# Storing x^T of a block in 384-byte pieces, reading low words on VectorE and sharing one set of buffers in an attention-and-softplus kernel

## The chip, the core and the metric

The kernel runs on one core of a Trainium2 chip. The metric is the device time of one execution in microseconds (us). Before the change it is 929.13 us, the median of three runs (928.65 to 930.0). The profile below is of another execution of the same kernel, with a span of 926.7 us from the first to the last instruction.

## The reference

Two blocks follow each other. The first is linear attention with a norm over each head; the second is a feed-forward layer with softplus between its two products.

```python
# q, k, v: (8 batches, 8 heads, 576 tokens, 64), g_norm: (64,)
kv  = einsum('bhsd,bhse->bhde', k, v)
o   = einsum('bhsd,bhde->bhse', q, kv)
o   = o / sqrt(mean(o * o, axis=-1) + 1e-6) * g_norm
x   = o.transpose(0, 2, 1, 3).reshape(4608, 512)
# moe_w_in: (512, 2048), moe_w_out: (2048, 512)
h   = x @ moe_w_in
g   = maximum(h, 0) + log1p(exp(-abs(h)))
out = g @ moe_w_out              # (4608, 512), float32
```

The weights arrive as 64-bit numbers (`wide` in the code): each is a low and a high 32-bit word, which the kernel turns into one float32.

## The kernel before

TensorE multiplies in a reduced float format (`F32R`), so each operand is divided into three parts (`[:, 0]`, `[:, 1]`, `[:, 2]`), and every product is a sum of three. The 4608 tokens are 12 blocks of 384 tokens, each three tiles of 128. The 2048 hidden columns are 16 chunks of 128. One step is one chunk of one block: 12 matmuls of 384 columns (`mm1`), softplus on ScalarE, a division of the result on ScalarE and VectorE, and 9 matmuls of 512 columns (`mm2`). There are 192 steps in three phases; in each phase a block takes only some of the chunks, because only 8 chunks' weights are resident, and a partial sum per tile goes to DRAM between phases.

No scheduler orders the instructions at run time: the Python class `Plan` lays every task on its engine's queue beforehand, from a guessed duration, a position (`pos`, in steps) and rings of buffers. A task that needs a buffer is put where the plan expects one to be free. The table `P0` holds the tuned positions. Where the plan expects a gap on TensorE before the first step, it puts a matmul that is thrown away (`warm`).

```python
    rings = dict(xv=2, gv=2, g=2, raw=2, lf=1, sq=1, t=1, p=1, w=1,
                 tail0=1, tail1=1, xt=2, kvt=6, qa=1, qT=2, x=2, xg=2, r=2,
                 h=2, o=2, tp=1, s0=1, s1=1, s2=1)
    # weight(): one weight tile of 128 x 512 numbers of two words each
            a1 = add("ACT", 670, square, [f], pos, [sq], [raw])
            a2 = add("ACT", 670, low, [f], pos, [lf], [raw])       # L289: lf <- low words
            d1 = add("DVE", 430, high1, [f], pos, [t], [raw])      # L292
            d2 = add("DVE", 690, high2, [d1], pos, [], [raw])      # L296
            d3 = add("DVE", 690, mask, [d2, a1], pos, [])          # L301
            ...
            d4 = add("DVE", 430, power, [d3], pos, [p, w])         # L309
            d5 = add("DVE", 690, rest, [d4, a2], pos, [], [lf])    # L314: p <- lf * p
            ready = add("DVE", 690, total, [d3, d5], pos, [], [t, p])  # L317
    # divide(): the weight's three parts; for the first chunks the third by TensorE (L368, L369)
    # split(): three parts of a tile of x^T, for mm1
        def high():                                                # L438, ACT
            nc.scalar.activation(cols(0, F32R), x.tile, func=AF.Identity, scale=g_down)
        def low():                                                 # L441, DVE
            nc.vector.scalar_tensor_tensor(out=cols(1, F32R), in0=x.tile, scalar=g_col, in1=cols(0), ...)
        def less():                                                # L445, DVE
            ...
    # kv_of(b): four pieces and a tail of k and v; L491 loads k, L493 v, L483/L485 the tails; L507 matmuls
    # load_q(b): from batch 2 on, q comes in runs of 128 bytes (L416), turned by VectorE (L554);
    # in batches 0 and 1 it comes in rows (L569) and is turned by TensorE (L579)
    # rows(t): attention of tile t
        a = o_task = add("PE", ..., out_rows, ...)                 # L524: o <- kv_diag, qT
        a = add("ACT", 600, <Square of o>, [a], pos, [x])          # L592
        a = add("DVE", 690, reduce, [a], pos, [r])                 # L529
        a = add("POOL", 2300, root, [a], pos)                      # L532, L533
        a = add("DVE", 700, norm, [a, o_task], pos, [], [o, r])    # L536
        if t < BY_PE:                                              # BY_PE = 12
            a = add("PE", 440, turn_x, [a], pos + 0.5, [xp], [x])  # L541
            if t < AT_ONCE:
                split(0, t, xp, a, pos + 0.5)
            ...                                                    # L601 copy, L602 store of x^T
            return
        def turn_blocks():                                         # L608: 32 x 32 blocks
            nc.vector.transpose(out=new(xg, [P, d_model]), in_=x.tile.rearrange("p h d -> p (h d)"))
        def store(r0):                                             # L611
            nc.sync.dma_start(out=xd[t][:, r0:r0 + BL].rearrange("(b i) j -> i b j", i=BL),
                              in_=xg.tile[r0:r0 + BL].rearrange("i (b j) -> i b j", j=BL))
        a = add("DVE", 690, turn_blocks, [a], pos, [xg], [x])
        x_there[t] = [add("SP", 450, lambda r0=r0: store(r0), [a], pos + 0.5, [], [xg], 450)
                      for r0 in range(0, P, BL)]
    # x_again(): x^T of a tile loaded from DRAM (L620) and split, in every phase
    # step(): mm1 L642, softplus L662, first part L664, second L653, third L657, mm2 L649
    # leave(): a tile's sum leaves its bank: L683 (phase 0) or L689, then a store L693
    # warm(): L747
```

Of the kernel before, what the change touches and what calls it, by code (L numbers as in the profile page):

```python
# [40 lines left out]
class Plan:  # L41
# [13 lines left out]
    def slot(self, ring):  # L55
        return Slot(ring)
# [10 lines left out]
    def order(self):  # L67
# [15 lines left out]
        while left:  # L83
            best = None
            for engine, tasks in ready.items():
                options = []
                for t in tasks:
                    at = max(engine_free[engine], t.ready)
                    if t.size:
                        at = max(at, dma_free - 2500)  # L90
                    for s in t.take:
                        if not free[s.ring]:
                            break
                        at = max(at, min(free[s.ring])[0])
# [47 lines left out]
def kernel(  # L142
# [41 lines left out]

    P0 = [-44.5, 1.3, -27.8, -10.7, -15.1, 4.5, -20.4, -2.8, -54.5, -31.8, -31.7, -9.2, -25.2, -1.2,
          27.3, -6.2, 3.0, -12.0, 8.5, 9.5, 5.0, 21.5, -1.5, 2.5, 2.5, 27.0, -6.5, 13.0, 9.0, 44.5,
          49.5, 67.5, 56.5, 71.5, 95.5, 100.5, 115.0, 112.0, 116.5, 9.0]
    CONVERT, FETCH, EARLY, LATER = P0[:8], P0[8:16], P0[16:27], P0[27:]
# [21 lines left out]

    rings = dict(xv=2, gv=2, g=2, raw=2, lf=1, sq=1, t=1, p=1, w=1,
                 tail0=1, tail1=1, xt=2, kvt=6, qa=1, qT=2, x=2, xg=2, r=2,
                 h=2, o=2, tp=1, s0=1, s1=1, s2=1)
# [44 lines left out]
    def weight(j, pos, fetch_pos):  # L258
# [8 lines left out]
        c, of_out = divmod(j, 2)  # L267
        raw, w = slot("raw"), slot("w")
        words = 2 if wide else 1
# [8 lines left out]
        if wide:  # L278
            sq, lf, t, p = (slot(n) for n in ("sq", "lf", "t", "p"))

# [3 lines left out]
            def square():  # L284
                nc.scalar.activation(new(sq, [P, d_model], BF16), raw.tile.bitcast(BF16)[:, :, 3],
                                     func=AF.Square, scale=2.0 ** 47)

            def low():
                nc.scalar.activation(new(lf, [P, d_model]), words_of()[0], func=AF.Copy, scale=2.0 ** -52)  # L289

# [21 lines left out]
            def rest():  # L312
                pf = p.tile.bitcast(F32)
                nc.vector.tensor_tensor(out=pf, in0=lf.tile, in1=pf, op=ALU.mult)  # L314

# [4 lines left out]
            a1 = add("ACT", 670, square, [f], pos, [sq], [raw])  # L320
            a2 = add("ACT", 670, low, [f], pos, [lf], [raw])
            d1 = add("DVE", 430, high1, [f], pos, [t], [raw])
# [3 lines left out]
            d4 = add("DVE", 430, power, [d3], pos, [p, w])  # L326
            d5 = add("DVE", 690, rest, [d4, a2], pos, [], [lf])
            ready = add("DVE", 690, total, [d3, d5], pos, [], [t, p])
# [3 lines left out]
        if c < PLACES or first_step[c] - last_step[c - PLACES] > 12:  # L332
            divide(j, w, ready, pos, "p", c < 4)
        else:
            spilled = dram.tile([P, d_model], F32, name=f"w_spill{j}")
            st = add("SP", 350, lambda: nc.sync.dma_start(out=spilled, in_=w.tile), [ready], pos, [], [w], 900)
            again = slot("x" if of_out else "qT")
# [3 lines left out]
            divide(j, again, ld, back, "xg")  # L341

# [54 lines left out]
    first_tile = [b * S // P for b in range(B)]  # L397
    xd = [dram.tile([d_model, P], F32, name=f"x{t}") for t in range(n_tiles)]
    x_there = {}
# [6 lines left out]
    def load_q(b):  # L406


        q_slots[b], q_loads[b] = slot("qa"), []
        pos = x_pos(first_tile[b] + 1) - EARLY[7]  # L410

        def run(e, c):
            if not (e or c):
                new(q_slots[b], [P, NP * S])
            r0 = BL * (2 * e + c)
            nc.sync.dma_start(  # L416
                out=q_slots[b].tile[r0:r0 + BL].rearrange("j (i d) -> j i d", d=BL),
                in_=q[b, e * NP:(e + 1) * NP, :, BL * c:BL * (c + 1)].rearrange("p (i j) d -> j (p i) d", j=BL))

        for e in range(2):  # L420
            for c in range(2):
                q_loads[b].append(add("SP", 450, lambda e=e, c=c: run(e, c), (), pos + 0.2 * (2 * e + c),
                                      [q_slots[b]] if not (e or c) else [], [], 2000, behind=int(pos) - 3,
                                      follows=q_loads[b][-1] if e or c else None))
# [41 lines left out]
    def kv_of(b):  # L466
# [5 lines left out]
        for p in range(NP + 1):  # L472
            tail = p == NP
            ks, vs = (slot(f"tail{i}" if tail else "kvt") for i in range(2))
            n = S - MAIN if tail else P

            def load(src, s, p=p, tail=tail, n=n, ks=ks):
# [14 lines left out]
                else:  # L492
# [3 lines left out]
                       620 if tail else size, behind=int(pos - 2) - 3)  # L496
                   for src, s, ns, size in ((k, ks, 900, 1250), (v, vs, 500, 900))]

# [18 lines left out]
    def rows(t):  # L517
        pos = x_pos(t)
        tp, qT, o, x, r, xp, xg = (slot(n) for n in ("tp", "qT", f"s{t}" if t < TB else "o", "x", "r", "tp", "xg"))
        def out_rows():  # L520
# [28 lines left out]
        for b, r0, n, s0 in parts(t):  # L549
# [12 lines left out]
            at_qa = n == P and b == 0  # L562
            q_s = q_slots[0] if at_qa else slot("kvt")

# [32 lines left out]
        if t < BY_PE:  # L597
            a = add("PE", 440, turn_x, [a], pos + 0.5, [xp], [x])
            if t < AT_ONCE:
                split(0, t, xp, a, pos + 0.5)  # L600
            a = add("ACT", 600, lambda: nc.scalar.copy(new(xg, [P, KD, P]), xp.tile), [a], pos + 1, [xg], [xp])  # L601
            x_there[t] = [add("SP", 450, lambda: nc.sync.dma_start(  # L602
                out=xd[t].rearrange("(a p) t -> p a t", p=P), in_=xg.tile), [a], pos + 1, [], [xg], 950)]
            return


        def turn_blocks():
            nc.vector.transpose(out=new(xg, [P, d_model]), in_=x.tile.rearrange("p h d -> p (h d)"))  # L608

        def store(r0):  # L610
            nc.sync.dma_start(out=xd[t][:, r0:r0 + BL].rearrange("(b i) j -> i b j", i=BL),  # L611
                              in_=xg.tile[r0:r0 + BL].rearrange("i (b j) -> i b j", j=BL))

        a = add("DVE", 690, turn_blocks, [a], pos, [xg], [x])
        x_there[t] = [add("SP", 450, lambda r0=r0: store(r0), [a], pos + 0.5, [], [xg], 450) for r0 in range(0, P, BL)]

    def x_again(ph, t):
        pos = first_step[ph, t // TB] - EARLY[8] + 0.5 * (t % TB)
        xt = slot("xt")
        ld = add("SP", 350, lambda: nc.sync.dma_start(out=new(xt, [P, KD, P]), in_=xd[t].rearrange("(a p) t -> p a t", p=P)),  # L620
                 x_there[t], pos - EARLY[9], [xt], [], 900, behind=first_step[ph, t // TB] - 5)
        split(ph, t, xt, ld, pos)
# [56 lines left out]
    def leave(ph, t, bank, done, pos):  # L679

        ot = slot("xg" if ph == 0 else ("qT", "x", "xg")[t % TB] if ph == LAST else "qT")
        if ph == 0:
            a = add("ACT", 600, lambda: nc.scalar.activation(new(ot, [P, d_model]), bank.tile, func=AF.Copy, scale=1.0 + E),  # L683
                    [done], pos, [ot], [bank])
        else:
            pt = slot("kvt")
            ld = add("SP", 350, lambda: nc.sync.dma_start(out=new(pt, [P, d_model]), in_=part[ph - 1, t][0]),
                     [part[ph - 1, t][1]], pos - EARLY[10], [pt], [], 900, behind=int(pos) - 4)
            a = add("DVE", 700, lambda: nc.vector.scalar_tensor_tensor(  # L689
                out=new(ot, [P, d_model]), in0=bank.tile, scalar=(scale if ph == LAST else 1.0 + E), in1=pt.tile,  # L690
                op0=ALU.mult, op1=ALU.add), [done, ld] + (scale_done if ph == LAST else []), pos, [ot], [bank, pt])
        dst = out[t * P:(t + 1) * P] if ph == LAST else dram.tile([P, d_model], F32, name=f"part{ph}_{t}")
        st = add("SP", 350, lambda: nc.sync.dma_start(out=dst, in_=ot.tile), [a], pos, [], [ot], 900)  # L693
        part[ph, t] = dst, st

    def whole_scale(pos):

        if not wide:
            scale_done.append(add("DVE", 60, lambda: nc.vector.memset(scale, 1.0 + E), (), pos))
            return  # L700
        ones, total = slot("kvt"), slot("h")
        a = add("DVE", 130, lambda: nc.vector.memset(new(ones, [P, P]), 1.0), (), pos, [ones])
# [80 lines left out]
```

## Time and profile before

| what | value |
|---|---|
| device time, median of 3 | 929.13 us |
| span of the profiled execution | 926.7 us |
| TensorE clock granted | 1.000 |
| mm1, L642 | 2304 matmuls, first at 46.6 us |
| mm2, L649 | 1728 matmuls |
| thrown-away matmuls, L747 | 48, 17.9 us busy, all before 46.6 us |
| low words, L289 on ScalarE | 32, 666 ns each |
| x^T by 32 x 32 blocks, L608 on VectorE | 24, 709 ns each |
| its stores, L611 | 96 DMAs of 64 KB |
| DMA packets | 265219, of which 164289 under 512 B |

The names: PE is TensorE, PEld its loading of weights, DVE VectorE, ACT ScalarE, POOL GpSimd and SP (or SPq) the queue that issues the DMAs. A line such as `L642` is a line of the kernel before. In the page's second part the span is cut into 40 slices of 23.2 us, and a digit is the busy share of one slice in tenths. The page's fifth part has one row for each group of equal instructions: how many, their busy time in all, the mean length of one in nanoseconds, and the idle time of the engine just before them with what ended it. In a timeline each row is one instruction or a run of equal ones, with its start and its length in microseconds, and in brackets the idle time before it and what ended that.

Matmuls are pipelined, so the lengths of neighbours overlap, and the sum of their busy times can't be read as the time that they need.

### The profile page before, as it was taken

The numbers are of one execution on the slowest core, as the hardware profiler recorded it, in microseconds if no ns is written. First come the engines' busy times: TensorE is split into PE (matmuls) and PEld (weight loads), VectorE is DVE, ScalarE is ACT, GpSimd is POOL, SyncE is SP. The second block draws the span as 40 slices with busy tenths as digits, with TensorE's granted clock in tenths as the row PEclk, the third lists the DMA queues.
The fourth block names the chain that finished last, engine by engine and source line by source line (L and its number), as shares of the span: only waits on it lengthen the run. The fifth ranks groups of instructions, "written<-read, shape, count | busy, mean of one in ns | idle before, by whom it ended". The sixth has DMA issues, their size and how long they took to land.

```text
span 926.7 us, 13338 instructions
## 1 busy us (share of the span) xinstructions
PE 909.2 (98%) x4826; PEld 818.4 (88%) x4826; DVE 628.2 (68%) x1055; ACT 433.7 (47%) x831; POOL 83.6 (9%) x78
## 2 busy tenths in 40 slices
PE   7899999999999999999999999999999999999998
PEld 5689888998998999998989999999889999999997
DVE  6865877876466786888855877888644455555553
ACT  6865654553334555655533555657323233323231
POOL 0322332221122220000000000000000000000000
PEclk9999999999999999999999999999999999999999
DMA  8998989794976452454534434544221323333322
GB/s 227 245 203 225 155 205 198 186 194 111 167 164 145 103 147 81 159 160 159 163 122 135 127 125 147 171 155 144 84 85 57 103 95 122 114 102 103 103 80 103
DMA packets 265219, 131.44 MB, mean 142 GB/s; under 512 B 164289, under 2 KB 239041, under 8 KB 265153
## 3 DMA queue, kind: packets, MB, share of 16 engines
q1 hardware_dynamic: 264992, 130.59, 54.3%
q8 instruction: 38, 0.62, 0.3%
q14 instruction: 29, 0.23, 0.1%
q10 hardware_dynamic: 160, 0.00, 0.0%
HBM read 91.75 MB, written 38.80 MB: 141 GB/s over the span
## 4 chain that ended last, share of the span: by engine, by line
PE 88%; DMA 6%; SPq 2%; DVE 1%; ACT 1%; issue 1%; POOL 0%; ACTq 0%; DVEq 0%
PE s L649 41%; PE h L642 41%; PE o L524 3%; PE o L507 3%; DMA kvt<-in_v_dram 2%; DMA xt<-x 1%; SPq L611 1%; DMA qa<-in_q_dram 1%; DMA part<-xg 1%; DMA raw<-in_moe_w_in_dram 1%; SPq L416 0%; DMA g_col<-in_g_norm_dram 0%; PE h L747 0%; PE tp L541 0%; PE tp L579 0%
## 5 line engine op out<-in xcount | busy, mean ns | idle before, releaser
L649 PE MATMUL s<-w,gv 128*128 128x512 f32 x1728 | 435.1, 395 | 1.0 <-ACT xg L683 0.9
L642 PE MATMUL h<-xv,w 128*128 128x384 f32 x2304 | 434.1, 337 | 0.0
L642 PEld LDWEIGHTS h<-xv,w 128*128 128x128 f32 x2304 | 406.3, 188 | 14.7
L649 PEld LDWEIGHTS s<-w,gv 128*128 128x128 f32 x1728 | 319.1, 188 | 61.4 <-ACT xg L683 2.6
L662 ACT ACTIVATE g<-h 128x384 f32<-128x384 f32 x192 | 94.1, 490 | 336.3 <-PE h L642 335.3
L653 DVE TENSOR_TENSOR gv<-g,gv 128x384 fp32r<-128x384 f32 x192 | 106.5, 555 | 170.0 <-ACT gv L664 169.1
L664 ACT ACTIVATE gv<-g 128x384 fp32r<-128x384 f32 x192 | 100.8, 525 | 40.3 <-PE s L649 33.1
L657 DVE SCALAR_TENSOR_TENSOR gv<-gv 128x384 fp32r<-128x384 f32 x192 | 106.9, 557 | 6.2
L441 DVE SCALAR_TENSOR_TENSOR xv<-xt,g_col,xv 128x512 fp32r<-128x512 f32 x102 | 75.8, 744 | 5.4 <-ACT xv L438 5.3
L438 ACT ACTIVATE xv<-xt,g_down 128x512 fp32r<-128x512 f32 x102 | 72.3, 713 | 10.6 <-DMA xt<-x 10.4
L445 DVE SCALAR_TENSOR_TENSOR xv<-xv 128x512 fp32r<-128x512 f32 x108 | 74.4, 689 | 2.6
L533 POOL TENSOR_TENSOR r<-r,half 128x8 f32<-128x8 f32 x36 | 68.0, 1888 | 3.0
L507 PEld LDWEIGHTS o<-kvt,kvt 128*128 128x128 f32 x256 | 33.4, 196 | 9.3 <-issue 6.8
L507 PE MATMUL o<-kvt,kvt 128*128 128x128 f32 x256 | 35.3, 282 | 6.3 <-DMA kvt<-in_v_dram 6.2
L524 PE MATMUL o<-kv_diag,qT 128*128 128x128 f32 (+1 forms) x296 | 37.5, 277 | 1.1 <-DVE x L536 1.1
L524 PEld LDWEIGHTS o<-kv_diag,qT 128*128 128x128 f32 (+1 forms) x296 | 35.0, 179 | 3.7 <-PE o L507 1.4
L532 POOL TENSOR_SCALAR r<-r 128x8 f32<-128x8 f32 x36 | 14.9, 414 | 249.0 <-DVE r L529 248.9
L689 DVE SCALAR_TENSOR_TENSOR qT<-s,kvt 128x512 f32<-128x512 f32 x36 | 24.6, 686 | 11.6 <-PE s L649 11.1
L554 DVE STREAM_TRANSPOSE qT<-qa 128x512 f32<-128x512 f32 (+1 forms) x30 | 19.0, 646 | 18.0 <-DMA qa<-in_q_dram 7.6
L529 DVE TENSOR_REDUCE r<-x 128x8 f32<-128x512 f32 x36 | 24.4, 678 | 8.3 <-ACT x L592 8.3
L689 DVE SCALAR_TENSOR_TENSOR qT<-s,scale,kvt 128x512 f32<-128x512 f32 x12 | 9.0, 751 | 29.7 <-PE s L649 29.7
L592 ACT ACTIVATE x<-o 128x512 f32<-128x512 f32 x33 | 19.7, 596 | 20.2 <-PE o L524 20.2
(74 smaller groups left out, 484.8 us busy)
## 6 DMA issues: line engine op xcount, KB each, us to landing
xt<-x SPq DMA_DIRECT2D x102, 256.0 KB, 3.4
kvt<-part SPq DMA_DIRECT2D x72, 256.0 KB, 3.9
part<-xg SPq DMA_DIRECT2D x36, 256.0 KB, 3.3
part<-qT SPq DMA_DIRECT2D x36, 256.0 KB, 2.3
raw<-in_moe_w_in_dram SPq DMA_DIRECT2D x16, 512.0 KB, 5.6
kvt<-in_k_dram SPq DMA_DIRECT2D x64, 128.0 KB, 3.7
kvt<-in_v_dram SPq DMA_DIRECT2D x32, 256.0 KB, 3.9
raw<-in_moe_w_out_dram SPq DMA_DIRECT2D x16, 512.0 KB, 4.5
```

Of the source, the lines that this page charges most:

```text
L438: nc.scalar.activation(cols(0, F32R), x.tile, func=AF.Identity, scale=g_down)
L441: nc.vector.scalar_tensor_tensor(out=cols(1, F32R), in0=x.tile, scalar=g_col, in1=cols(0), op0=ALU.mult, op1=ALU.subtract)
L445: nc.vector.scalar_tensor_tensor(out=cols(2, F32R), in0=cols(1), scalar=-RADIX, in1=cols(0), op0=ALU.mult, op1=ALU.add)
L507: nc.tensor.matmul(kv[:, i if tail else p], lhsT=l, rhs=r, start=(p == 0 and i == 0), stop=tail, skip_group_check=True)
L524: nc.tensor.matmul(y[r0:r0 + n, p::NP], lhsT=qT.tile[:, p, r0:r0 + n], rhs=kv_diag[b % 2][:, p].rearrange("r (h d) -> r h d", d=D), start= ...
L533: nc.gpsimd.tensor_tensor(out=r.tile, in0=r.tile, in1=half, op=ALU.pow)
L642: nc.tensor.matmul(hp, lhsT=w_in.tile[:, i, kd * P:(kd + 1) * P], rhs=xv.tile[:, i, kd], start=(m == 0), stop=(m == 3 * KD - 1))
L649: nc.tensor.matmul(mine[i].tile, lhsT=gv.tile[:, m, i * P:(i + 1) * P], rhs=w_out.tile[:, m], start=(c == cs[0] and m == 0), stop=(c == cs ...
L653: nc.vector.tensor_tensor(out=gv.tile[:, 1], in0=g.tile, in1=gv.tile.bitcast(F32)[:, 0], op=ALU.subtract)
L657: nc.vector.scalar_tensor_tensor(out=gv.tile[:, 2], in0=f32[:, 1], scalar=-RADIX, in1=f32[:, 0], op0=ALU.mult, op1=ALU.add)
L662: a = add("ACT", 490, lambda: nc.scalar.activation(new(g, [P, NT]), h.tile, func=AF.Softplus, scale=1.0 + E), [a], s, [g], [h])
L664: a = add("ACT", 530, lambda: nc.scalar.activation(new(gv, [P, 3, NT], F32R)[:, 0], g.tile, func=AF.Copy, scale=DOWN), [a], s, [gv])
```

## The change

It has four parts.

1. From tile 12 on, the three transposed tiles of a block are gathered in one buffer (`xb`), and stored when the third is there. A row of x^T in DRAM then holds the tokens of its block in another order, so that one contiguous piece is 3 x 32 numbers, 384 bytes, where it was 128. x^T is now one DRAM tensor for each block. Since the tokens of such a block stand in another order in all later products, a tile of the result has rows of three places, and its store puts them back with two DMAs.
2. The low words are no longer converted by ScalarE into a buffer `lf`; VectorE's operation `rest` reads them from `raw` directly and does the scaling in the same pass.
3. The rings lf, t, p, w, xt, kvt, qT and xg (16 buffers together) become one ring `m` of 13 buffers; the planner can now give two buffers of one ring to a task.
4. The table of positions `P0` and some guessed durations are set anew, so that instructions stand in another order.

```diff
-    P0 = [-44.5, 1.3, -27.8, -10.7, -15.1, 4.5, -20.4, -2.8, -54.5, -31.8, ...
+    P0 = [-93.0, -6.2, -50.8, -8.7, -11.6, -1.5, -14.9, 2.7, -53.5, -34.8, ...
...
-    rings = dict(xv=2, gv=2, g=2, raw=2, lf=1, sq=1, t=1, p=1, w=1,
-                 tail0=1, tail1=1, xt=2, kvt=6, qa=1, qT=2, x=2, xg=2, r=2,
+    rings = dict(m=13, xv=2, gv=2, g=2, raw=2, sq=1, 
+                 tail0=1, tail1=1, qa=1, xb=1, x=2, r=2,
...
-            def low():
-                nc.scalar.activation(new(lf, [P, d_model]), words_of()[0], func=AF.Copy, scale=2.0 ** -52)
...
-                nc.vector.tensor_tensor(out=pf, in0=lf.tile, in1=pf, op=ALU.mult)
+                nc.vector.scalar_tensor_tensor(out=pf, in0=words_of()[0], scalar=2.0 ** -52, in1=pf,
+                                               op0=ALU.mult, op1=ALU.mult)
...
-            d5 = add("DVE", 690, rest, [d4, a2], pos, [], [lf])
+            d5 = add("DVE", 690, rest, [d4], pos, [], [raw])
...
-    xd = [dram.tile([d_model, P], F32, name=f"x{t}") for t in range(n_tiles)]
+    xd = [dram.tile([d_model, NT], F32, name=f"x{n}") for n in range(n_blocks)]
...
         def turn_blocks():
-            nc.vector.transpose(out=new(xg, [P, d_model]), in_=x.tile.rearrange("p h d -> p (h d)"))
+            if i == 0:
+                new(xb, [P, d_model // BL, TB, BL])
+            nc.vector.transpose(out=xb.tile[:, :, i], in_=x.tile.rearrange("p h d -> p (h d)").rearrange(
+                "p (b j) -> p b j", j=BL))
 
-        def store(r0):
-            nc.sync.dma_start(out=xd[t][:, r0:r0 + BL].rearrange("(b i) j -> i b j", i=BL),
-                              in_=xg.tile[r0:r0 + BL].rearrange("i (b j) -> i b j", j=BL))
+        def store(a):
+            nc.sync.dma_start(out=xd[n][:, a * TB * BL:(a + 1) * TB * BL].rearrange("(b i) m -> i b m", i=BL),
+                              in_=xb.tile[a * BL:(a + 1) * BL].rearrange("i b t j -> i b (t j)"))
...
+        if i == TB - 1:
+            stores = [add("SP", 450, lambda a=a: store(a), turns, pos + 0.5, [], [xb], 820) for a in range(P // BL)]
...
+        if ph == LAST and t >= BY_PE:
+            n, i = divmod(t, TB)
+            def store():
+                m = 0
+                while m < P // BL:
+                    a, u = divmod(P // BL * i + m, TB)
+                    k = min(TB - u, P // BL - m)
+                    nc.sync.dma_start(
+                        out=out[n * NT:(n + 1) * NT].rearrange("(t s) f -> t s f", t=TB)[u:u + k, a * BL:(a + 1) * BL],
+                        in_=ot.tile[m * BL:(m + k) * BL])
+                    m += k
```

More of the change, by code (lines that the diff above doesn't have):

```diff
@@ L90, in order @@
                         at = max(at, dma_free - 2500)
-                    for s in t.take:
-                        if not free[s.ring]:
+                    for i, s in enumerate(t.take):
+                        others = sum(u.ring == s.ring for u in t.take[:i])
+                        if len(free[s.ring]) <= others:
                             break
-                        at = max(at, min(free[s.ring])[0])
+                        at = max(at, sorted(free[s.ring])[others][0])
                     else:
@@ L183 @@
     LAST = PHASES[-1]
-    P0 = [-44.5, 1.3, -27.8, -10.7, -15.1, 4.5, -20.4, -2.8, -54.5, -31.8, -31.7, -9.2, -25.2, -1.2,
-          27.3, -6.2, 3.0, -12.0, 8.5, 9.5, 5.0, 21.5, -1.5, 2.5, 2.5, 27.0, -6.5, 13.0, 9.0, 44.5,
-          49.5, 67.5, 56.5, 71.5, 95.5, 100.5, 115.0, 112.0, 116.5, 9.0]
+    P0 = [-93.0, -6.2, -50.8, -8.7, -11.6, -1.5, -14.9, 2.7, -53.5, -34.8, -51.7, -14.7, -24.2, 1.3,
+          -0.2, -4.2, 2.5, -13.0, 8.5, 9.5, 5.5, 23.5, -2.0, 2.5, 2.5, 7.0, 5.0, 14.5, 9.0, 44.5, 49.5,
+          68.5, 52.5, 72.0, 95.5, 100.5, 114.5, 111.0, 116.5, 8.5]
     CONVERT, FETCH, EARLY, LATER = P0[:8], P0[8:16], P0[16:27], P0[27:]
@@ L267, in weight @@
         c, of_out = divmod(j, 2)
-        raw, w = slot("raw"), slot("w")
+        raw, w = slot("raw"), slot("m")
         words = 2 if wide else 1
@@ L278, in weight @@
         if wide:
-            sq, lf, t, p = (slot(n) for n in ("sq", "lf", "t", "p"))
+            sq, t, p = (slot(n) for n in ("sq", "m", "m"))
             def words_of():
@@ L320, in weight @@
             a1 = add("ACT", 670, square, [f], pos, [sq], [raw])
-            a2 = add("ACT", 670, low, [f], pos, [lf], [raw])
             d1 = add("DVE", 430, high1, [f], pos, [t], [raw])
@@ L332, in weight @@
         if c < PLACES or first_step[c] - last_step[c - PLACES] > 12:
-            divide(j, w, ready, pos, "p", c < 4)
+            divide(j, w, ready, pos, "m", c < 4)
         else:
@@ L336, in weight @@
             st = add("SP", 350, lambda: nc.sync.dma_start(out=spilled, in_=w.tile), [ready], pos, [], [w], 900)
-            again = slot("x" if of_out else "qT")
+            again = slot("x" if of_out else "m")
             back = max(last_step[c - PLACES] + 0.5, first_step[c] - 3)
@@ L340, in weight @@
                      [st], back, [again], [], 900, behind=last_step[c - PLACES] - 1)
-            divide(j, again, ld, back, "xg")
+            divide(j, again, ld, back, "m")
     def divide(j, w, ready, pos, ring, by_pe=False):
@@ L397 @@
     first_tile = [b * S // P for b in range(B)]
-    xd = [dram.tile([d_model, P], F32, name=f"x{t}") for t in range(n_tiles)]
+    xd = [dram.tile([d_model, NT], F32, name=f"x{n}") for n in range(n_blocks)]
+    xb_slots = {}
     x_there = {}
@@ L422, in load_q @@
                 q_loads[b].append(add("SP", 450, lambda e=e, c=c: run(e, c), (), pos + 0.2 * (2 * e + c),
-                                      [q_slots[b]] if not (e or c) else [], [], 2000, behind=int(pos) - 3,
+                                      [q_slots[b]] if not (e or c) else [], [], 2190, behind=int(pos) - 3,
                                       follows=q_loads[b][-1] if e or c else None))
@@ L473, in kv_of @@
             tail = p == NP
-            ks, vs = (slot(f"tail{i}" if tail else "kvt") for i in range(2))
+            ks, vs = (slot(f"tail{i}" if tail else "m") for i in range(2))
             n = S - MAIN if tail else P
@@ L496, in kv_of @@
                        620 if tail else size, behind=int(pos - 2) - 3)
-                   for src, s, ns, size in ((k, ks, 900, 1250), (v, vs, 500, 900))]
+                   for src, s, ns, size in ((k, ks, 900, 1300), (v, vs, 500, 850))]
             def run(ks=ks, vs=vs, p=p, tail=tail, n=n):
@@ L518, in rows @@
         pos = x_pos(t)
-        tp, qT, o, x, r, xp, xg = (slot(n) for n in ("tp", "qT", f"s{t}" if t < TB else "o", "x", "r", "tp", "xg"))
+        tp, qT, o, x, r, xp, xg = (slot(n) for n in ("tp", "m", f"s{t}" if t < TB else "o", "x", "r", "tp", "m"))
         def out_rows():
@@ L562, in rows @@
             at_qa = n == P and b == 0
-            q_s = q_slots[0] if at_qa else slot("kvt")
+            q_s = q_slots[0] if at_qa else slot("m")
             def load(b=b, n=n, s0=s0, q_s=q_s, at_qa=at_qa):
@@ L602, in rows @@
             x_there[t] = [add("SP", 450, lambda: nc.sync.dma_start(
-                out=xd[t].rearrange("(a p) t -> p a t", p=P), in_=xg.tile), [a], pos + 1, [], [xg], 950)]
+                out=x_of(t), in_=xg.tile), [a], pos + 1, [], [xg], 1000)]
             return
+        n, i = divmod(t, TB)
+        if i == 0:
+            xb_slots[n] = slot("xb"), []
+        xb, turns = xb_slots[n]
         def turn_blocks():
-            nc.vector.transpose(out=new(xg, [P, d_model]), in_=x.tile.rearrange("p h d -> p (h d)"))
@@ L610, in store @@
-        def store(r0):
-            nc.sync.dma_start(out=xd[t][:, r0:r0 + BL].rearrange("(b i) j -> i b j", i=BL),
-                              in_=xg.tile[r0:r0 + BL].rearrange("i (b j) -> i b j", j=BL))
-        a = add("DVE", 690, turn_blocks, [a], pos, [xg], [x])
-        x_there[t] = [add("SP", 450, lambda r0=r0: store(r0), [a], pos + 0.5, [], [xg], 450) for r0 in range(0, P, BL)]
+            if i == 0:
+                new(xb, [P, d_model // BL, TB, BL])
+            nc.vector.transpose(out=xb.tile[:, :, i], in_=x.tile.rearrange("p h d -> p (h d)").rearrange(
+                "p (b j) -> p b j", j=BL))
@@ new lines, in store @@
+        def store(a):
+            nc.sync.dma_start(out=xd[n][:, a * TB * BL:(a + 1) * TB * BL].rearrange("(b i) m -> i b m", i=BL),
+                              in_=xb.tile[a * BL:(a + 1) * BL].rearrange("i b t j -> i b (t j)"))
+        turns.append(add("DVE", 710, turn_blocks, [a], pos, [] if i else [xb], [x], follows=turns[-1] if i else None))
+        if i == TB - 1:
+            stores = [add("SP", 450, lambda a=a: store(a), turns, pos + 0.5, [], [xb], 820) for a in range(P // BL)]
+            for u in range(n * TB, t + 1):
+                x_there[u] = stores
@@ L617, in x_again, with x_of @@
+    def x_of(t):
+        n, i = divmod(t, TB)
+        return xd[n][:, i * P:(i + 1) * P].rearrange("(a p) t -> p a t", p=P)
     def x_again(ph, t):
         pos = first_step[ph, t // TB] - EARLY[8] + 0.5 * (t % TB)
-        xt = slot("xt")
-        ld = add("SP", 350, lambda: nc.sync.dma_start(out=new(xt, [P, KD, P]), in_=xd[t].rearrange("(a p) t -> p a t", p=P)),
-                 x_there[t], pos - EARLY[9], [xt], [], 900, behind=first_step[ph, t // TB] - 5)
+        xt = slot("m")
+        ld = add("SP", 350, lambda: nc.sync.dma_start(out=new(xt, [P, KD, P]), in_=x_of(t)),
+                 x_there[t], pos - EARLY[9], [xt], [], 1000, behind=first_step[ph, t // TB] - 5)
@@ L679, in leave @@
     def leave(ph, t, bank, done, pos):
-        ot = slot("xg" if ph == 0 else ("qT", "x", "xg")[t % TB] if ph == LAST else "qT")
+        ot = slot("m" if ph == 0 else ("m", "x", "m")[t % TB] if ph == LAST else "m")
         if ph == 0:
@@ L685, in leave @@
         else:
-            pt = slot("kvt")
+            pt = slot("m")
             ld = add("SP", 350, lambda: nc.sync.dma_start(out=new(pt, [P, d_model]), in_=part[ph - 1, t][0]),
@@ L691, in leave @@
                 op0=ALU.mult, op1=ALU.add), [done, ld] + (scale_done if ph == LAST else []), pos, [ot], [bank, pt])
+        if ph == LAST and t >= BY_PE:
+            n, i = divmod(t, TB)
+            def store():
[7 more added lines that the diff above has]
+                    m += k
+            part[ph, t] = None, add("SP", 800, store, [a], pos, [], [ot], 750)
+            return
         dst = out[t * P:(t + 1) * P] if ph == LAST else dram.tile([P, d_model], F32, name=f"part{ph}_{t}")
-        st = add("SP", 350, lambda: nc.sync.dma_start(out=dst, in_=ot.tile), [a], pos, [], [ot], 900)
+        st = add("SP", 350, lambda: nc.sync.dma_start(out=dst, in_=ot.tile), [a], pos, [], [ot], 720)
         part[ph, t] = dst, st
@@ L700, in whole_scale @@
             return
-        ones, total = slot("kvt"), slot("h")
+        ones, total = slot("m"), slot("h")
         a = add("DVE", 130, lambda: nc.vector.memset(new(ones, [P, P]), 1.0), (), pos, [ones])
```

## The prediction, made before the changed kernel was run

> **What bounds the kernel now.** I read the page first, then the table of windows, the waits of TensorE, and last the timelines of TensorE, ScalarE and VectorE around the first wide product. From the page (share of the span by engine, and the slices in tenths):
>
> ```profile
> PE 909.2 (98%) x4826; PEld 818.4 (88%) x4826; DVE 628.2 (68%) x1055; ACT 433.7 (47%) x831; POOL 83.6 (9%) x78
> ...
> PE   7899999999999999999999999999999999999998
> ...
> DMA  8998989794976452454534434544221323333322
> ```
>
> TensorE is busy in nearly every slice; no other engine is. The DMA row is at 8 or 9 only in the first third. Busy time of pipelined matmuls says little of the rate, so the windows (columns: PE, PEld, DVE, ACT, POOL busy, clock, DMA share, GB/s):
>
> ```profile
> 0.00:20.00 20.00, 14.59 (x58) 10.37 (x59) 13.01 (x27) 11.78 (x21) 0.69 (x6) 1.00 0.84 224
> 20.00:40.00 20.00, 17.97 (x109) 13.50 (x108) 17.74 (x29) 17.33 (x34) 7.31 (x6) 1.00 0.99 239
> 40.00:60.00 20.00, 18.65 (x125) 16.16 (x124) 15.41 (x26) 13.99 (x28) 5.37 (x7) 1.00 1.07 203
> ...
> 800.00:900.00 100.00, 100.00 (x503) 90.57 (x502) 55.99 (x92) 33.12 (x62) 0.00 (x0) 1.00 0.35 112
> ```
>
> A step is 12 matmuls of mm1 and 9 of mm2. 503 / 21 = 23.95 steps in 100 us, 4.175 us a step; 192 steps are 801.6 us. The change leaves every one of them alone. So 926.7 - 801.6 = 125.1 us is all there is to win from: 46.6 us until the first mm1, about 4 us of tail, and 74.5 us in between of attention work on TensorE and waits. The waits it has there are short:
>
> ```profile
> PE o L507 <- DMA kvt<-in_v_dram: 6.2, 4, 3.0
> ...
> PE o L524 <- DVE x L536: 1.1, 2, 0.9
> PE tp L541 <- ACT gv L664: 0.9, 1, 0.9
> PE s L649 <- ACT xg L683: 0.9, 3, 0.5
> ```
>
> Of the first line only 1.7 us (at 62.7 us) falls after the first mm1, so the named waits after it are 1.7 + 1.1 + 0.9 + 0.9 = 4.6 us. The start is the larger part. The timelines of TensorE, then ScalarE, then VectorE there (start, length, then what ended the idle time before it):
>
> ```profile
> 41.05 0.63 PE L541 MATMUL tp<-ident_r,x 128*128 128x128 f32 x4 [0.51 <-DVE x L536]
> ...
> 43.41 1.16 PE L507 MATMUL o<-kvt,kvt 128*128 128x128 f32 x8 [0.84 <-DMA kvt<-in_v_dram]
> 44.41 1.06 PE L507 MATMUL o<-tail,tail 128*128 128x128 f32 x8
> ...
> 46.57 2.35 PE L642 MATMUL h<-xv,w 128*128 128x384 f32 x12
> ```
>
> ```profile
> 42.67 0.67 ACT L285 ACTIVATE sq<-raw 128x512 bf16<-128x512 bf16 x1 [1.97 <-DMA raw<-in_moe_w_in_dram]
> 43.24 0.66 ACT L289 ACTIVATE lf<-raw 128x512 f32<-128x512 uint32 x1
> 43.80 0.67 ACT L438 ACTIVATE xv<-tp,g_down 128x512 fp32r<-128x512 f32 x1
> ```
>
> ```profile
> 44.98 0.75 DVE L441 SCALAR_TENSOR_TENSOR xv<-tp,g_col,xv 128x512 fp32r<-128x512 f32 x1 [0.30 <-ACT xg L601]
> 45.76 0.69 DVE L445 SCALAR_TENSOR_TENSOR xv<-xv 128x512 fp32r<-128x512 f32 x1
> ```
>
> The last split of block 0 ends at 46.45 and mm1 starts at 46.57: that chain sets the start. Its transpose was done at 41.7, but ScalarE stood 1.97 us before a weight that had not landed, then did its two passes, and only then the split. VectorE idled less than 3 us between 9.0 and 46.4 us: it is nearly the bound there.
>
> **What the Trainium skill says.** "Perfetto Trace Analysis", section "Identifying the Most-Contended Engine", calls matmul busy time a bad measure of headroom, because matmuls are pipelined. The trace agrees: PE is 1.00 busy in every late window and still the true measure is 4.175 us a step. The same page, "Optimization Strategy", says that repeated gaps on the engine that should be full can mean too few buffers. Here it is partly so: the loads of v wait 12.4 us in five waits until TensorE lets a kvt buffer go (waits of the DMA queue), but TensorE pays for only one of them after the start. "VectorE: DVE Perf Modes", in its perf-mode tier table, puts fp32 tensor_tensor at one element a cycle. The trace shows the same time for both two-source forms, L314 690 ns and L296 (which reads the weights' words at a stride of 8 bytes) 688 ns; so the new form of L314 should cost the same. "DMA: Bandwidth & Descriptors", section "Specifications", gives 512 B as the least transfer for line rate. 164289 of 265219 packets are under 512 B; 40 to 60 us, where q comes in runs of 128 B, moves 203 GB/s at a share of 1.07 against 239 at 0.99 just before: it agrees.
>
> **The change part by part.**
>
> *Low words.* 32 ScalarE passes (L289, 666 ns, 21.3 us) vanish. Seven lie before the first mm1: 7 x 0.666 = 4.7 us of ScalarE there. VectorE gets no extra instruction. The cost is that the raw buffer is held longer, until VectorE's fifth operation.
>
> *Shared buffers.* Sixteen buffers of eight rings (lf, t, p, w, xt, kvt, qT, xg) become 13 that anyone takes, and one of three tiles for x^T. A load of v or q no longer needs a kvt buffer in particular.
>
> *Order.* The new positions move instructions. In the changed program, 49 VectorE instructions run from the first weight to the last split of block 0, where 56 did. Gone from before it: one whole weight (0.422 + 0.688 + 0.686 + 0.424 + 0.690 + 0.690 = 3.60 us) and three operations of a second (0.422 + 0.688 + 0.686 = 1.80). New before it: one reduction (0.678) and one norm (0.685). Net 5.40 - 1.36 = 4.0 us less, so the split ends near 42.4. On ScalarE that split now stands ahead of the weight that blocked it. By DMA: the second batch's last k and v end at 9.96 MB of issued bytes before, and TensorE had them at 43.4 us, 229 KB a us; in the changed program it is 8.91 MB, so 38.9 us. Then 0.85 of kv, 0.42 turn, 0.70, 0.75 and 0.69 for the split and 0.4 of handovers: 42.7. Two ways agree: first mm1 near **42.7**, 3.9 earlier, with one more transpose (0.4) already behind it. TensorE agrees roughly: 43 filling matmuls (L747) stand before the first mm1 instead of 48, each 0.3 to 0.5 us.
>
> Not all of it stays. The weights put off must still be converted, and k and v of batch 2 must still land; TensorE then waits where it waited before. I give back a third of 4.3: 2.9 stays.
>
> *Batch 2.* The 128-byte loads of q for it (four of 288 KB, issued 40.9 to 58.7 us) now follow its k and v instead of preceding them. Of the 1.7 us wait at 62.7 I count 0.7 as won.
>
> *x^T.* 24 tiles went out as 96 issues of 64 KB in 128 B runs, 49152 packets; now 32 issues of 192 KB in 384 B runs, 16384 packets. The store waits for the block's third tile. All this lies at 121 to 340 us, beside steps: TensorE waits there under 2.9 us (all of the last list but the 1.7), so at most that; I count 1.3.
>
> *Stores of the result.* For tiles from 12 on, two DMAs instead of one, a third more work on a queue with room. After the last VectorE result the queue issues twice (0.33 us each) instead of once: 0.35 us on the end.
>
> Sum: 2.9 + 0.7 + 1.3 - 0.35 = 4.55 us. 929.13 - 4.55 = 924.6.
>
> **Rivals.** *The work put off comes back as a wait*: three weights are converted while the first products run; VectorE is 15.4 of 20 us busy there, and mm2 of chunks 2 and 3 needs them. Then nothing of the start stays: 928. *The DMA stays the bound*: its share is about 1 up to 200 us. If the shared buffers let loads run ahead and delay those needed first, TensorE waits more: 930 to 932. *It was hidden anyway*: ScalarE is 47% busy and x^T is off the path, so only the order counts; this is my main line. *The start collapses to the chain*: filling work and waits together are over 20 us of the first 46.6; if all three engines profit, the first mm1 comes at 39 or 40 and nothing is given back: 919.
>
> **Range and chances.** 924.6 in the middle; 919 if the start keeps all and the later waits go, 930 if a new wait eats it. Two per cent is 18.6 us: it needs a first mm1 near 28 us, sooner than 229 KB a us can bring two batches; 0.03. Slower by 2% would need new waits four times those named; 0.02.
>
> **What would show it.** First mm1 (mm1's matmul row) between 41.5 and 44 us; the step late in the run still 4.17 to 4.18; the new low-word operation 680 to 700 ns; waits of TensorE after the first mm1 under 4 us; packets down by about 33000; DMA share at 100 to 200 us below 0.95; tail 0.2 to 0.5 longer. I am wrong if the first mm1 comes at 43 and the span is still above 926: then look for a wait on a weight or on k and v between 45 and 110 us. Wrong too if mm1 starts later than 45.

## The result and the profile after

The changed kernel takes 934.29 us (median of 6 runs, 933.51 to 935.19), the kernel before 928.45 us in the same comparison: a ratio of 1.0063, with an interval of 1.005 to 1.0076. It is slower by 0.6%, and outside the predicted range. From the page of the changed kernel, the rows shown of before, the clock and the packets:

```profile
PE 904.9 (97%) x4821; PEld 818.5 (88%) x4821; DVE 627.3 (67%) x1055; ACT 414.5 (44%) x799; POOL 80.4 (9%) x78
...
PE   7899999999999999999999999999999999999992
...
PEclk8999999999999999999999999999999999999997
DMA  8999998498782554346334445551231233444321
...
DMA packets 231377, 131.43 MB, mean 141 GB/s; under 512 B 130448, under 2 KB 205200, under 8 KB 231312
```

Two digits matter. The last slice of PE was 8 and is 2: TensorE has finished, and 16 us of the span are left. The first digit of the clock is 8; in the kernel before the granted clock was 1.000 throughout. Now the end, as timelines: TensorE in the changed kernel and then in the kernel before, and the changed kernel's DMA queue:

```profile
911.89 4.37 PE L665 MATMUL s<-w,gv 128*128 128x512 f32 x18
```

```profile
918.35 4.37 PE L649 MATMUL s<-w,gv 128*128 128x512 f32 x18
```

```profile
915.69 1.21 SPq L716 DMA_DIRECT2D out_dram<-m  x2
...
917.01 1.53 SPq L716 DMA_DIRECT2D out_dram<-x  x2
918.64 1.29 SPq L716 DMA_DIRECT2D out_dram<-m  x2
```

The last matmul ends at 916.3 us; before the change it ended at 922.7. TensorE is 6.4 us *earlier*. The last store is issued by 919.9, and then the queue waits 11.6 us for it (the DMA queue's own waits):

```profile
SPq L809 <- DMA out_dram<-m: 11.6, 1, 11.6
```

The windows say how it lands. First the changed kernel, then the kernel before (the last two columns are the mean share of the 16 DMA engines, and GB/s; the third from the end is TensorE's clock):

```profile
918.00:920.00 2.00, 0.00 (x0) 0.00 (x0) 0.00 (x0) 0.00 (x0) 0.00 (x0) 0.81 0.46 78
...
924.00:926.00 2.00, 0.00 (x0) 0.00 (x0) 0.00 (x0) 0.00 (x0) 0.00 (x0) 0.50 0.13 37
...
928.00:930.00 2.00, 0.00 (x0) 0.00 (x0) 0.00 (x0) 0.00 (x0) 0.00 (x0) 0.50 0.13 51
```

```profile
923.00:924.00 1.00, 0.00 (x0) 0.00 (x0) 0.51 (x1) 0.00 (x0) 0.00 (x0) 1.00 0.97 361
924.00:925.00 1.00, 0.00 (x0) 0.00 (x0) 0.00 (x0) 0.00 (x0) 0.00 (x0) 1.00 1.05 389
```

A share of 0.13 is two of sixteen engines, at 51 / 2 = 25 GB/s each; before, all sixteen ran, at 389 / 16 = 24 each. In the last stretch single engines are as fast as before, and fourteen have nothing to do. An estimate of the length: the last block has four pieces of 64 or 96 rows, and a piece of k x 32 rows that runs on k engines gives each of them 32 rows of 2 KB, 64 KB, or 2.6 us at 25 GB/s. If the four take the same two engines, one behind the other, that is 10.5 us, near the queue's 11.6. The trace doesn't name the engines, so this isn't shown; nor is why the share at 918 to 920 us is 0.46 at only 78 GB/s. The tail, from the last matmul to the end, is 932.7 - 916.3 = 16.4 us against 4.0. In sum 12.4 - 6.4 = 6.0 us, which is the difference of the spans, 932.7 - 926.7. These are single traces. By their ratios, two versions below without the slow end are 3.9 and 4.8 us faster than the kernel before, so TensorE's gain is better read as 4 to 6 us, and the cost of the end as 10 to 12.

### The profile page after: what moved, and what is told of

It is laid out like the page before. It is cut to its first block, busy times and chain, and to the rows that moved or that the text cites. A ratio compares the mean times of both kernels' runs of the same rounds, so it can differ in the third digit from the quotient of the medians.

```text
span 932.7 us, 13257 instructions
## 1 busy us (share of the span) xinstructions
PE 904.9 (97%) x4821; PEld 818.5 (88%) x4821; DVE 627.3 (67%) x1055; ACT 414.5 (44%) x799; POOL 80.4 (9%) x78
## 4 chain that ended last, share of the span: by engine, by line
PE 93%; SPq 2%; DVE 1%; DMA 1%; POOL 1%; ACT 1%; issue 0%; ACTq 0%
PE s L665 43%; PE h L658 43%; PE o L523 3%; PE o L506 3%; SPq L568 1%; DMA g_col<-in_g_norm_dram 1%; PE tp L540 0%; POOL r L532 0%; DMA m<-in_v_dram 0%; DMA qa<-in_q_dram 0%; DVE m L312 0%; PE tp L578 0%; DVE r L528 0%; DVE xv L440 0%; DVE m L316 0%
## 5 line engine op out<-in xcount | busy, mean ns | idle before, releaser
L440 DVE SCALAR_TENSOR_TENSOR xv<-m,g_col,xv 128x512 fp32r<-128x512 f32 x102 | 75.8, 743 | 1.1 <-ACT xv L437 1.1
L437 ACT ACTIVATE xv<-m,g_down 128x512 fp32r<-128x512 f32 x102 | 69.7, 710 | 2.5 <-DMA m<-x 2.4
L506 PEld LDWEIGHTS o<-m,m 128*128 128x128 f32 x256 | 34.2, 200 | 8.7 <-issue 7.3
L506 PE MATMUL o<-m,m 128*128 128x128 f32 x256 | 35.4, 285 | 6.4 <-DMA m<-in_v_dram 6.4
L705 DVE SCALAR_TENSOR_TENSOR m<-s,scale,m 128x512 f32<-128x512 f32 x24 | 17.9, 747 | 29.7 <-PE s L665 29.7
L523 PE MATMUL o<-kv_diag,m 128*128 128x128 f32 (+1 forms) x296 | 36.9, 275 | 0.0
L523 PEld LDWEIGHTS o<-kv_diag,m 128*128 128x128 f32 (+1 forms) x296 | 35.0, 179 | 1.8 <-issue 1.0
L535 DVE TENSOR_TENSOR x<-o,r 128x512 f32<-128x512 f32 x33 | 22.7, 688 | 17.6 <-POOL r L532 17.6
L705 DVE SCALAR_TENSOR_TENSOR m<-s,m 128x512 f32<-128x512 f32 x36 | 23.3, 684 | 10.2 <-PE s L665 10.1
L286 ACT ACTIVATE sq<-raw 128x512 bf16<-128x512 bf16 x32 | 21.3, 665 | 16.4 <-DMA raw<-in_moe_w_in_dram 10.2
```

Of the source, the lines that this page charges most:

```text
L506: nc.tensor.matmul(kv[:, i if tail else p], lhsT=l, rhs=r, start=(p == 0 and i == 0), stop=tail, skip_group_check=True)
L523: nc.tensor.matmul(y[r0:r0 + n, p::NP], lhsT=qT.tile[:, p, r0:r0 + n], rhs=kv_diag[b % 2][:, p].rearrange("r (h d) -> r h d", d=D), start= ...
```

## The experiments

Of each run the time is given with its ratio to the kernel before, which ran beside it at 926.9 to 927.2 us.

**Stores of 32 rows.** Only the stores change; TensorE, VectorE and ScalarE have the changed kernel's order.

```diff
-                    k = min(TB - u, P // BL - m)
+                    k = 1
...
-    ...rearrange("(t s) f -> t s f", t=TB)[u:u + k, a * BL:(a + 1) * BL],
+    ...rearrange("(t s) f -> t s f", t=TB)[u, a * BL:(a + 1) * BL],
```

> The changed kernel, with its last stores cut finer: each tile from 12 on goes out as four DMAs of 32 rows x 512, where it was two with an outermost dimension of 2 or 3. No other instruction changes its place. Theory A (a store whose outermost dimension is 2 or 3 runs on that many of the 16 DMA engines; the trace shows a share of 0.13 and 51 GB/s at 926 to 930 us): the last matmul stays at 916.3 us, the tail falls from 16.4 us to 6 us or less (12 issues of about 0.35 us, then about 2 us of landing), the time is 922 to 925. Rival B (the tail comes from the stores being small, or from work heaped up in the queue by the new order): twice as many and smaller DMAs leave it at 932 to 938.

Measured: 924.94 us, ratio 0.9978 (0.9971 to 0.9985). The last matmul ends at 916.2, as predicted, and the tail is 7.3 us, 1.3 over A's limit, because each issue takes about 0.45 us and not 0.35 (the queue's timeline):

```profile
915.62 1.72 SPq L716 DMA_DIRECT2D out_dram<-m  x4
...
919.32 1.79 SPq L716 DMA_DIRECT2D out_dram<-m  x4
```

More and smaller DMAs are about 8 us better (ratio 0.9978 where it was 1.0063), so neither their number nor their size was the cost.

**The same sizes, two dimensions.** Each piece of 32, 64 or 96 rows goes to consecutive rows (the result has its rows in another order).

```diff
-    out=out[n * NT:(n + 1) * NT].rearrange("(t s) f -> t s f", t=TB)[u:u + k, a * BL:(a + 1) * BL],
+    out=out[t * P + m * BL:t * P + (m + k) * BL],
```

> The changed kernel, with the same number of stores of the same sizes, but each piece written to consecutive rows as 32, 64 or 96 rows x 512 (two dimensions), so the rows of the result stand in another order. Theory A: the tail falls to 4 to 5 us, the time is 921 to 923. Rival B (two unequal pieces are what costs, whatever their shape): 932 to 935.

Measured: 924.75 us, ratio 0.9969 (0.9956 to 0.9982). In its trace the last matmul ends at 917.3 and the tail is 5.7 us, some above A's figures and far from B's. The number and sizes of the stores are the changed kernel's; only the outer dimension of the destination is gone, and with it about 9 us (ratio 0.9969 where it was 1.0063).

**The pieces in the kernel before.** Its stores from tile 12 on get the changed kernel's form, with all else in its place (rows of the result in another order).

```diff
+        if ph == LAST and t >= BY_PE:
+            ...                                  # for each piece of k tokens, as in the changed kernel
+                    nc.sync.dma_start(
+                        out=...rearrange("(t s) f -> t s f", t=TB)[u:u + k, a * BL:(a + 1) * BL],
+                        in_=ot.tile[m * BL:(m + k) * BL])
```

> The kernel before, with only its last stores changed: each tile from 12 on goes out in the changed kernel's two pieces with outermost dimension 1, 2 or 3, so the rows of the result stand in another order; no other instruction changes its place. Theory A: the tail grows from 4.0 us to about 16 us with the last matmul still near 922.7, so the time is 938 to 942. Rival B (the heaped queue of the new order): the old order has no such heap, the time stays within 929 to 931.

Measured: 977.92 us, ratio 1.0554 (1.0532 to 1.0576). The tail is 16.4 us, as A says, and B falls. But the last matmul ends at 959.2 us, and the time is 51 us longer and not 12: both theories missed this. The waits from 700 us on show where much of the rest lies:

```profile
ACT g L662 <- PE h L642: 130.2, 40, 6.5
ACT xv L438 <- DMA xt<-x: 56.3, 6, 9.6
...
PE s L649 <- ACT gv L664: 22.8, 6, 4.0
```

ScalarE stands six times 9 us before a piece of x^T for the next block, behind it the softplus, and behind that TensorE. TensorE's own waits for ScalarE and VectorE there add up to 25.8 us. The clock takes more: in windows of 20 us it falls to 0.83 to 0.97 in seven windows between 780 and 940 us, which, if work slows in proportion, is an estimated 12 us. With the 12.4 of the tail that accounts for the 51. In the kernel before two buffers hold x^T, so a third tile's load is issued only after the block's slow stores (at 781.8 us, behind stores issued from 774.9 on), and it lands late. In the changed kernel all three loads of a block are issued together ahead of the stores (its queue's timeline):

```profile
862.71 5.85 SPq L636 DMA_DIRECT2D m<-x  x3
875.89 1.23 SPq L716 DMA_DIRECT2D out_dram<-m  x2
877.61 1.18 SPq L716 DMA_DIRECT2D out_dram<-x  x2
```

So the new buffers and order, as it seems, hid seven blocks of slow stores; the eighth has nothing behind which to hide. The next run tests this.

**Only the last block plain.** Tiles 33 to 35 keep the old layout of x^T and a plain store; blocks 4 to 10 are as in the changed kernel, and TensorE's order is too.

```diff
+    PLAIN = 33
...                        # from tile PLAIN on, the kernel before's transpose and stores of x^T
-        if ph == LAST and t >= BY_PE:
+        if ph == LAST and BY_PE <= t < PLAIN:
```

> The changed kernel, with only its last block (tiles 33 to 35) in the old layout of x^T and with plain stores of 128 rows; blocks 4 to 10 keep the pieces of 384 bytes and the stores with an outermost dimension of 1, 2 or 3. TensorE's order is the changed kernel's. Theory A (the slow stores cost only where nothing is left to do beside them): the seven blocks' slow stores stay hidden, the tail falls from 16.4 to 4.7 us, the time is 922 to 923. Rival (the queue is filled by the slow stores of block 10, and the last plain stores land behind them): the tail is 8 us or more, 925 to 930.

Measured: 923.08 us, ratio 0.9958 (0.9943 to 0.9973). The tail is 3.8 us. Slow stores in the middle cost nothing that shows here; the loss was the last block's.

**The old x^T.** Parts 2 to 4 of the change without part 1.

```diff
-    xd = [dram.tile([d_model, NT], F32, name=f"x{n}") for n in range(n_blocks)]
+    xd = [dram.tile([d_model, P], F32, name=f"x{t}") for t in range(n_tiles)]
...
-            in_=xb.tile[a * BL:(a + 1) * BL].rearrange("i b t j -> i b (t j)"))
+            in_=xg.tile[r0:r0 + BL].rearrange("i (b j) -> i b j", j=BL))
...
-        if ph == LAST and t >= BY_PE:
+        if False:                                # a plain store for every tile
```

> The changed kernel without its first part: x^T in pieces of 128 bytes, a store per tile as soon as it is turned, the plain store of the result; low words on VectorE, the shared buffers and the new positions stay. Theory A for the tail: 4 us as in the kernel before. For the 6.4 us by which TensorE ends earlier, two theories. P (the order and the shared buffers win it, x^T is off the path): the last matmul stays at 916 to 917, the time is 921 to 923. Q (fewer small packets win it): TensorE waits again 3 to 5 us between 100 and 340 us, the time is 925 to 928.

Measured: 922.62 us, ratio 0.9948 (0.9934 to 0.9963). The last matmul ends at 915.4 (916 to 917 was expected), and the tail is 4.7 us. TensorE's waits from 46 to 350 us, here and then in the changed kernel:

```profile
PE tp L578 <- DVE xv L440: 0.7, 1, 0.7
PE o L506 <- DMA m<-in_v_dram: 0.5, 1, 0.5
```

```profile
PE o L506 <- DMA m<-in_v_dram: 1.3, 1, 1.3
PE tp L578 <- DVE xv L440: 0.7, 1, 0.7
```

Before there were 4.6 us of them. With or without the pieces of 384 bytes they are gone, so theory P holds: 33842 packets fewer won TensorE nothing that shows.

**Low words on ScalarE again**, in the version with the old x^T.

```diff
+            a2 = add("ACT", 670, low, [f], pos, [lf], [raw])
...
-            d5 = add("DVE", 690, rest, [d4], pos, [], [raw])
+            d5 = add("DVE", 690, rest, [d4, a2], pos, [], [lf])
```

> The version with the old x^T (922.6 us), and the low words converted by ScalarE again, into a buffer of the shared ring: 32 more ScalarE passes of 666 ns, seven of them before the first wide product; the planner moves some neighbours. Theory P (the order and the buffers win the 6 us, ScalarE is not what sets the start): within 1 us of 922.6. Theory Q (the freed ScalarE time sets the start): the first mm1 comes 2 to 4 us later and the time is 924.5 to 927.

Measured: 927.17 us, ratio 0.9998 (0.9989 to 1.0007): all that the version had won is lost, which is Q. The first mm1 comes 2.2 us later than without (48.6 against 46.4), and one chunk then waits for its weight:

```profile
PE h L649 <- ACT w L373: 3.4, 1, 3.4
```

The planner also moved neighbours here, and each low-word buffer takes one of the 13 shared ones, so this is the worth of part 2 within this order, not of 32 passes alone.

**The start.** The first mm1 had hardly moved (46.4 us against 46.6). ScalarE's beginning in the changed kernel (at L743 it multiplies g_norm by a constant; ACT_TABLE_LOAD is a load of its function table):

```profile
7.01 1.28 ACT L743 ACT_TABLE_LOAD   x1 [7.01 <-DMA g_col<-in_g_norm_dram]
...
8.52 1.28 ACT L744 ACT_TABLE_LOAD   x1
...
10.03 0.64 ACT L286 ACTIVATE sq<-raw 128x512 bf16<-128x512 bf16 x1
```

Before, its first weight began at 8.34. Half a megabyte of a second weight now stands in the queue ahead of k, v, and g_norm's 256 bytes land 1.7 us later; everything behind them on ScalarE shifts. TensorE's first kv matmul moved from 7.5 to 9.1 us, and around its wait the clock was halved (windows of the changed kernel, the clock is the third figure from the end):

```profile
8.00:12.00 4.00, 2.95 (x11) 2.63 (x12) 1.22 (x3) 3.20 (x6) 0.00 (x0) 0.50 1.09 244
12.00:16.00 4.00, 3.12 (x11) 2.27 (x11) 3.90 (x7) 2.50 (x6) 0.00 (x0) 0.66 0.59 161
```

Three runs, all on the version with the old x^T, take away the early weight and ScalarE's wait for g_norm, singly and together. In that version the clock is halved too, but later, from 17 to 21 us. The first run moves one load, the second one small product:

```diff
-    ... -53.5, -34.8, -51.7, ...        # FETCH of the weights 0, 1, 2
+    ... -53.5, -33.4, -34.3, ...
```

```diff
         def high():
+            if not g_down_done:
+                nc.scalar.mul(g_down, g_col, DOWN_G)
+                g_down_done.append(1)
             nc.scalar.activation(cols(0, F32R), x.tile, func=AF.Identity, scale=g_down)
...
-    nc.scalar.mul(g_down, g_col, DOWN_G)
+    g_down_done = []
```

> The version with the old x^T, with one load moved: the second weight is fetched after the first k and v instead of before them, as the kernel before had it; two fillers move, nothing else. Theory S (the start lost what the order promised because 0.5 MB more weights stand ahead of k, v and of g_norm): the first kv matmul comes at 7.5 us instead of 9.3, the matmul clock isn't halved at 8 to 14 us, the first mm1 comes 1 to 2 us earlier, the time is 920.5 to 921.8. Rival T (the DMA moves the same bytes before the first mm1 in any order): no change, 922 to 923.

> The version with the old x^T, with the product g_norm x constant moved from the head of ScalarE's queue to just before its first use, so that the table load and the first weight's pass no longer wait for g_norm's small load (7.6 us); one table load fewer, nothing else moves. Theory S2 (ScalarE's late beginning, 10.6 us against 8.3 us before the change, delays the chain of weights and with it the first mm1): ScalarE begins its first weight near 6 us, the first mm1 comes 2 to 4 us earlier, the time is 919 to 921. Rival T (DMA sets the first mm1): ScalarE and VectorE only wait later, 922 to 923.

> Both of the moves of the start in the version with the old x^T. If S and S2 hold and don't overlap, 918 to 920; if they shorten the same chain, as the better of the two alone; under T 922 to 923.

Measured: 919.91 us, ratio 0.9915 (0.990 to 0.993); 919.62 us, 0.9913 (0.9898 to 0.9928); both together 919.76 us, 0.9913 (0.9898 to 0.9928). The mm1 row of the three, in this order (shortest, median and longest in ns, then first and last start in us):

```profile
L646 PE MATMUL h<-xv,w x2304: 332/336/447, 44.5 to 908.6; 128*128 128x384 f32 x192
```

```profile
L649 PE MATMUL h<-xv,w x2304: 332/336/448, 44.0 to 908.9; 128*128 128x384 f32 x192
```

```profile
L649 PE MATMUL h<-xv,w x2304: 332/336/445, 43.2 to 908.4; 128*128 128x384 f32 x192
```

The first mm1 comes 1.9 and 2.4 us earlier, as S and S2 said. In the first run the first kv matmul comes at 8.2 us, where S had 7.5, and the time is below S's 920.5. In the second ScalarE begins its first weight at 5.57 us, not at 10.6. The clock is not what they share: the first keeps 1.00 throughout, in the second it is 0.50 from about 9 to 12.5 us, and its mm1 is the earlier one. Together they bring 3.2, but the last matmul only moves from 913.1 and 913.4 to 912.9: TensorE then waits 1.0 us for v after the first mm1. These three are the fastest versions but for the last run below, which equals them; they can't be told apart.

T is right in one thing. The changed kernel's TensorE, at the last piece (the tail) of the second batch's k and v and at the first mm1:

```profile
42.46 1.05 PE L506 MATMUL o<-tail,tail 128*128 128x128 f32 x8
...
46.38 2.35 PE L658 MATMUL h<-xv,w 128*128 128x384 f32 x12
```

The version with the old x^T has 42.37 for that tail, and the three runs have 40.52, 40.01 and 39.32; the first mm1 follows 3.9 to 4.0 us later in all five. So both moves seem to act by letting those loads be issued sooner. The DMA queue's own waits fit: after the third v it stands 3.5 us in the changed kernel, and 3.8 with the old x^T, for a `raw` buffer that L312, the new low-word operation on VectorE, lets go; in the three runs it is 1.7 us, none and none.

**The table load in the kernel before**, the same small move.

```diff
         def high():
+            if not g_down_done:
+                nc.scalar.mul(g_down, g_col, DOWN_G)
+                g_down_done.append(1)
...
-    nc.scalar.mul(g_down, g_col, DOWN_G)
+    g_down_done = []
```

> The kernel before, with the product g_norm x constant moved from the head of ScalarE's queue to just before its first use; nothing else moves. If ScalarE's late beginning (8.3 us) sets the start in the old order as it does in the new one: first mm1 2 us earlier, the time 924.5 to 926. If the weight that ScalarE stands before at 40.7 to 42.7 us and the DMA set it there: no change, 926.5 to 928.

Measured: 925.66 us, ratio 0.9986 (0.9978 to 0.9995), the first mm1 at 45.6, one microsecond earlier and not two. The move is worth less in the old order, 1.3 us by the ratio.

**The last block plain, and k and v first.**

```diff
-    ... -53.5, -34.8, -51.7, ...        # FETCH of the weights 0, 1, 2
+    ... -53.5, -33.4, -34.3, ...
```

> The version with only the last block plain, and the second weight fetched after the first k and v. Against the version with the old x^T and the same load moved (919.9 us) it differs only in x^T's pieces of 384 bytes for blocks 4 to 10. If the fewer packets win nothing on TensorE: 919.5 to 920.5. If they win something hidden until now: below 919.

Measured: 919.75 us, ratio 0.9928 (0.9911 to 0.9944), against 919.91 with the old x^T throughout. Even with the better start, the pieces of 384 bytes in blocks 4 to 10 change nothing that can be seen.

## Why the prediction was wrong

- **Stores of the result** is the step that failed: "two DMAs instead of one", "0.35 us on the end". The cost was to be one more issue; the tail grew by 12.4 us instead, and the trace shows few DMA engines busy there. I counted issues and bytes and did not look at the shape. The Trainium skill, "DMA: Bandwidth & Descriptors", says under "Why a DMA increments its semaphore by 16 and not by 1" that the number of engines is the largest up to 16 that divides the slowest dimension, leaving out dimensions of size 1, of both sides. For a destination of 3 x 32 x 512 or 2 x 32 x 512 that gives 3 or 2. The measured share of 0.13 agrees with 2; the very last piece has 96 rows, for which it gives 3, and that only two engines are busy at the end would fit if the third, with no share in the pieces of 64 rows, was done sooner; this isn't shown. Flat pieces of the same sizes took the loss away. No rival of mine named the end of the kernel.
- **Order** (the start) was mis-sized: first mm1 foreseen at 42.7, 2.9 us of it kept; measured 46.4, 0.2 us. VectorE's work fell as summed: between 9.0 and 46.4 us it was busy 33.0 us before and 28.5 after. But its idle time rose from 4.4 to 8.9 us (it was not "less than 3 us" before), so less work did not bring an earlier end. The sum of bytes foresaw the second batch's k and v at 38.9 us; the last full piece came at 40.2 and the tail at 42.5, and the 3.9 us from there to mm1 are near the 3.8 of the sum. The step that failed here is the even 229 KB a us, which was 220 from 9.0 to 46.4 us, and 161 from 12 to 16: it left out the first 13 us, with the weight fetched too early, ScalarE behind a small load, and the queue before a `raw` buffer, a hold that "Low words" named and gave no cost. With the load and the product moved, that tail of k and v came at 39.3 and the first mm1 at 43.2. The sign set there, "wrong too if mm1 starts later than 45", came.
- **Batch 2** and **x^T** together were to bring 2.0. From first mm1 to last matmul TensorE took 876.1 us and now takes 869.9, 6.2 less: too small by 4.2, and the cause I gave for 1.3 of it, fewer packets, did not hold. The waits after the first mm1 fell from 4.6 to 2.0 us; the trace names no cause for the rest. It lies before 350 us: from 50 to 350 us TensorE begins 1755 matmuls where it began 1730, and from 350 to 900 us 2766 where it was 2767.
- **Low words**: the new operation takes 693 ns, within the 680 to 700 foreseen. I held the ScalarE time to be hidden ("only the order counts; this is my main line"). The run that put it back lost 4.5 us.
- Right were the step late in the run (503 matmuls in 100 us again), packets down by about 33000, and a DMA share below 0.95 at 100 to 200 us (0.97 and 0.75 in its halves, 0.86 in the mean).
- In numbers: -2.9 - 0.7 - 1.3 + 0.35 was foreseen, -0.2 - 6.2 + 12.4 came, in this pair of traces.

Open: how the 6.2 us divide between the shared buffers and the new positions; no run separates them.

## What to carry to other kernels

Read a store's shape, not only its bytes. Where the outermost dimension was 2 or 3, cutting the DMA into pieces of 32 rows, or keeping 32 to 96 rows outermost, took the loss away; look above all at the last store, which nothing hides. When a change is slower in sum, look first at when the bound engine ends: here it ended 6.4 us earlier, and the loss was all behind it. A start is a chain of its own: undoing either a wait for a 256-byte load at the head of an engine's queue or one weight fetched too early was worth about 3 us, and both together no more. Less work on an engine moves the end only if what it waits for comes earlier too.

## What was not expected of the hardware

Slow stores don't only land late. In the kernel before they held up loads issued behind them on the same queue, six times by 9.4 us on average, and the time rose by 51 us, four times the 12.4 us by which the tail grew. And near the changed kernel's wait of 3.4 us on TensorE at the start its clock was at 0.50 from about 8 to 14.7 us. The length of a wait alone does not decide this: with the second weight fetched later TensorE waited 3.6 us there, and the clock stayed at 1.00. No loss of time is shown for it at the start: with the old x^T it was halved from 17 to 21 us instead, and the first mm1 came at 46.4 us in both.
